# Two-block cached attention on one core: reciprocals by pairs of heads, K transposes behind them, another order of the PV evictions and exponentials, and a hinted branch at the end

## Chip, core and metric

The kernel runs on one core of a Trainium2 chip. The core has five engines: TensorE (PE; its weight loads are shown apart as PEld), VectorE (DVE), ScalarE (ACT), GpSimd (POOL) and SyncE (SP), and 16 DMA engines that move data between HBM and on-chip memory (SBUF). Results of TensorE land in PSUM, which has eight banks. The metric is the device time of one execution in microseconds (us). Before the change it is 743.23 us, the median of three runs (743.22 to 743.76).

## What is computed

Two blocks A and B of the same shape; each is a query projection, an attention over a cached K and V, and an output projection. The results stand side by side.

```python
def _A_ref(x, k_cache, v_cache, wq, wo):        # x 16x64x640, caches 16x32x512x128, wq 640x4096, wo 4096x640
    B, Sq, D = x.shape
    H, Dh = 32, 128
    q = (x @ wq).reshape(B, Sq, H, Dh).transpose(0, 2, 1, 3)
    scores = jnp.einsum("bhqd,bhkd->bhqk", q, k_cache) * (Dh ** -0.5)
    p = _softmax(scores, axis=-1)
    o = jnp.einsum("bhqk,bhkd->bhqd", p, v_cache)
    return o.transpose(0, 2, 1, 3).reshape(B, Sq, H * Dh) @ wo
...
return jnp.concatenate([a, b], axis=-1)          # 16 x 64 x 1280, bf16
```

## The kernel before

**Packs and phases.** The work is cut into 128 packs. A pack n is two batches (128 query rows) by four heads. Four packs make a group (16 heads of one pair of batches, sharing one transposed x and one accumulated output); eight groups (eight pairs of batches) make a phase; the four phases are block A heads 0 to 15, A heads 16 to 31, B heads 0 to 15, B heads 16 to 31. The last two packs are "narrow": their V is laid out in another way.

**The steps of one pack**, with the names that the planner uses: XT and XC (transpose of x, once per group), QP (query projection on PE, L610), QE (its eviction by ACT, L616), LDK and LDV (loads of K and V, issued by SP, L559 and L570), KT (two 32x32-block transposes of K by DVE, one for each half, L624), S (scores on PE, into the four PSUM banks 0 to 3, one for each head, L634), EX (exponential by ACT, one per head, which also writes the row sum, L653), RC (reciprocal of the row sums by DVE, L666), NM (normalisation of P by POOL, one per head, into `pn_sb`, L682), TR (transposes of P on PE, into banks 4 and 5, L693), TE (their eviction by DVE, one per bank, L703), PV (P times V on PE, into the first columns of banks 4 to 7, L716), OE (eviction of PV by ACT, in two halves: OE 0 reads banks 4 and 5, OE 1 reads banks 6 and 7, L724), ZO (ACT writes zeros over the part of banks 6 and 7 that PV used, L728), OP (output projection on PE, into the other columns of banks 6 and 7, L736), OS (DVE adds the group's sum, L746 and L749), ST (store of a finished group by ACT's queue, L755).

**What sets the order.** `build_plan` gives every step a due time in units of a pack, from the table `AT`; each engine's program is its steps sorted by due time. So one turn of PE is QP(n), PV(n-2), S(n), TR(n-1), OP(n-2), and DVE's turn before the change is

KT 0 (n), TE 0 (n-2), TE 1 (n-2), RC of heads 0 to 2 (n-1), KT 1 (n), RC of head 3 (n-1).

The loads on SP's queue are sorted by their own keys: V(n) is issued when PV(n-4) is done, since V has four buffers; K(m) has six buffers and stands about 2.5 packs further ahead. The waits between engines are worked out by the planner. Some steps of the other engines count on one semaphore that PE waits for (`for_pe`), and `stand_in` names, for every other dependence, a later step on the same engine whose completion covers it: before the change TR waits for the OE of banks 4 and 5, which stands second on ACT, and by that for both.

**The code on PE** is a loop over four packs; the other engines' programs are written out in full.

**The end.** The kernel computes the exponentials without subtracting the maximum. At the end DVE checks that all row sums are in range (FL1, FLM, FLC) and writes `flag`. Every engine loads the flag (L837) and branches (`If_ne`, L838): if it is not 128 the engine runs a second, general program, which lies behind the branch; otherwise it jumps over that program to the end, where ACT waits for the last store.

## Time and profile before

| what | value |
|---|---|
| median of three runs | 743.23 us |
| the profiled execution's own time | 743.14 us |
| its span, first to last instruction | 741.4 us |
| mean granted TensorE clock | 0.986 |
| busy DVE, ACT, POOL | 517.0, 519.8, 405.0 us |
| instructions | 61715 |
| DMA packets, bytes | 79841, 295.19 MB, mean 398 GB/s |

The span is the time that the trace covers; 1.7 us of the profiled execution's time lie around it. In the page, rows of busy shares cut the span into 40 equal slices (18.5 us each), a digit 9 standing for 90% or more. In the timeline, a row has the start and the length in us, the engine, the line of the kernel, the operation, output and input, and how many like instructions were merged; what stands in brackets is how long the engine was idle before and what released it. "SPq" is SP's queue, "PEldq" the sequencer of the engine.

### The profile page before, as it was taken

The page shows a single profiled execution, that of the slowest core. Times are in us where ns is not written, and L with a number is a line of the kernel's source. Part 1 is how long each engine was busy: PE and PEld are TensorE (multiplying, and loading weights), DVE is VectorE, ACT ScalarE, POOL GpSimd, SP SyncE. Part 2 cuts the span into 40 slices and gives each one's busy share as a digit, 9 for nine tenths or more (in the row PEclk, how much of TensorE's full clock was granted, in tenths as well). Part 3 has the DMA queues.
Part 4 walks back from the last instruction along what each step waited for, and adds up shares of the span by engine and source line. Part 5 has one row for each costly group of instructions (what it writes and reads, how often), then busy time and mean ns, then how long its engine had stood idle before and what let it go on. Part 6 is the DMA issues. An engine that isn't in the chain of part 4 may idle for free.

```text
span 741.4 us, 61715 instructions
## 1 busy us (share of the span) xinstructions
PE 680.6 (92%) x28502; PEld 532.2 (72%) x28502; DVE 517.0 (70%) x818; ACT 519.8 (70%) x1559; POOL 405.0 (55%) x580
## 2 busy tenths in 40 slices
PE   3679999999999999999988999999998899999995
PEld 2457777778787777777766777777776677777873
DVE  6347777778777776677755676677676677787874
ACT  1448787877777777776756777777776677777773
POOL 2635555555874544545674455455487455555551
PEclk9889999999999999999999999999999999999998
DMA  9999999999999999999999999999999999999980
GB/s 323 393 404 413 415 413 416 413 415 413 412 402 414 414 418 414 416 416 415 415 400 410 414 415 414 413 415 413 416 412 403 410 417 416 415 417 415 416 322 20
DMA packets 79841, 295.19 MB, mean 398 GB/s; under 512 B 13360, under 2 KB 28208, under 8 KB 63408
## 3 DMA queue, kind: packets, MB, share of 16 engines
q1 hardware_dynamic: 68384, 281.43, 93.9%
q10 hardware_dynamic: 11408, 13.27, 5.1%
q14 instruction: 39, 0.32, 0.1%
q8 instruction: 10, 0.16, 0.1%
HBM read 292.03 MB, written 2.62 MB: 397 GB/s over the span
## 4 chain that ended last, share of the span: by engine, by line
PE 45%; SPq 38%; DMA 7%; issue 4%; ACT 3%; POOL 2%; DVE 1%; ACTq 0%; DVEq 0%
SPq L559 24%; SPq L570 12%; PE ps L716 11%; PE ps L736 11%; PE ps L610 10%; PE ps L634 7%; PE ps L693 6%; DMA v_ring<-in_B_v_cache_dram 3%; DMA ws_sb<-in_A_wq_dram 2%; DMA kn_ring<-in_B_k_cache_dram 2%; ACT oT_sb L724 2%; SPq L544 1%; POOL pn_sb L682 1%; ACT ps L728 1%; POOL wqp_sb L582 1%
## 5 line engine op out<-in xcount | busy, mean ns | idle before, releaser
L682 POOL TENSOR_SCALAR pn_sb<-p_ring,recip 128x512 bf16<-128x512 bf16 x508 | 342.8, 696 | 304.1 <-DVE recip L666 304.1
L624 DVE STREAM_TRANSPOSE kt_ring<-kn_ring 128x1024 f32<-128x1024 f32 x256 | 312.0, 1227 | 105.3 <-DMA kn_ring<-in_B_k_cache_dram 69.7
L653 ACT ACTIVATE p_ring<-ps 128x512 bf16<-128x512 f32 x512 | 298.9, 598 | 35.3 <-issue 6.6
L703 DVE COPY pT_sb<-ps 128x1024 bf16<-128x1024 bf16 x258 | 164.4, 678 | 104.0 <-PE ps L693 103.5
L716 PE MATMUL ps<-pT_sb,v_ring 32*128 32x64 bf16 x16512 | 164.5, 192 | 18.6 <-DMA v_ring<-in_B_v_cache_dram 11.6
L716 PEld LDWEIGHTS ps<-pT_sb,v_ring 32*128 32x128 bf16 x16512 | 148.6, 91 | 34.0 <-DMA v_ring<-in_B_v_cache_dram 14.4
L610 PE MATMUL ps<-xT_ring,wqp_sb 128*128 128x128 bf16 x2560 | 165.8, 220 | 7.4 <-POOL xT_ring L599 7.1
L610 PEld LDWEIGHTS ps<-xT_ring,wqp_sb 128*128 128x128 bf16 x2560 | 157.2, 114 | 14.5 <-issue 7.3
L736 PE MATMUL ps<-wo_sb,oT_sb 128*128 128x320 bf16 x1040 | 166.3, 303 | 1.0 <-ACT ps L728 1.0
L724 ACT ACTIVATE oT_sb<-ps 128x256 bf16<-128x256 f32 x260 | 85.6, 381 | 108.9 <-PE ps L716 108.0
L634 PE MATMUL ps<-kt_ring,qs_ring 32*64 32x512 bf16 x4096 | 139.1, 382 | 3.7 <-issue 3.7
L693 PEld LDWEIGHTS ps<-ident,pn_sb 64*128 64x128 bf16 x4128 | 70.2, 95 | 76.6 <-ACT oT_sb L724 34.8
L616 ACT ACTIVATE qs_ring<-ps 128x512 bf16<-128x512 f32 x128 | 76.5, 598 | 62.3 <-PE ps L610 62.1
L736 PEld LDWEIGHTS ps<-wo_sb,oT_sb 128*128 128x128 bf16 x1040 | 92.0, 99 | 38.7 <-ACT ps L728 1.2
L653 ACT ACTIVATION_READ_ACCUMULATOR p_ring<-ps 128x1 f32 x512 | 106.1, 207 | 0.0
L693 PE MATMUL ps<-ident,pn_sb 64*128 64x64 bf16 x4128 | 84.1, 191 | 20.2 <-POOL pn_sb L682 6.7
L634 PEld LDWEIGHTS ps<-kt_ring,qs_ring 32*64 32x64 bf16 x4096 | 53.4, 103 | 32.1 <-issue 4.8
L728 ACT ACTIVATE ps<-zeros 128x256 f32<-128x256 bf16 x130 | 51.3, 394 | 0.0
L582 POOL COPY wqp_sb<-ws_sb 128x1280 bf16<-128x1280 bf16 x32 | 39.4, 1263 | 15.8 <-DMA ws_sb<-in_A_wq_dram 15.8
L666 DVE RECIPROCAL recip<-rowsum 128x3 f32<-128x3 f32 (+1 forms) x256 | 37.1, 145 | 5.3 <-ACT p_ring L653 0.7
L599 POOL COPY xT_ring<-xs_sb 128x640 bf16<-128x640 bf16 x32 | 23.1, 722 | 0.1
L589 PE MATMUL ps<-ident,xn_ring 128*128 128x128 bf16 x165 | 14.9, 222 | 3.9 <-DMA xn_ring<-in_A_x_dram 3.1
(26 smaller groups left out, 66.0 us busy)
## 6 DMA issues: line engine op xcount, KB each, us to landing
kn_ring<-in_A_k_cache_dram SPq DMA_DIRECT2D x256, 256.0 KB
v_ring<-in_A_v_cache_dram SPq DMA_DIRECT2D x128, 512.0 KB
kn_ring<-in_B_k_cache_dram SPq DMA_DIRECT2D x256, 256.0 KB
v_ring<-in_B_v_cache_dram SPq DMA_DIRECT2D x128, 512.0 KB
ws_sb<-in_B_wq_dram SPq DMA_DIRECT2D x10, 512.0 KB, 16.8
wo_sb<-in_B_wo_dram ACTq DMA_DIRECT2D x8, 640.0 KB, 13.5
ws_sb<-in_A_wq_dram ACTq DMA_DIRECT2D x4, 640.0 KB, 17.9
wo_sb<-in_A_wo_dram SPq DMA_DIRECT2D x4, 640.0 KB, 14.1
```

The source lines that it names most:

```text
L559: ins = e.dma_start(kn_ring[2 * b + l::4, n % NK].rearrange("p a c -> p (a c)"), src)
L570: ins = e.dma_start(dst.rearrange("p t d -> p (t d)"), src.rearrange("h (p t) d -> (h p) (t d)", t=16))
L610: last = e.matmul(ps[:, 1, f * 128:(f + 1) * 128], w[:, kt, f, :], xT_ring[:, xs, kt, :], start=(kt == 0), stop=(kt == KT - 1))
L624: ins = e.transpose(dst.rearrange("p c b (h l) -> p c h b l", h=8, l=2), src)
L634: last = e.matmul(ps[64 * b:64 * b + 64, i, :], qs_ring[rows, n % NQ, f, b, :], kt_ring[rows, n % NKT, :, f // 2, b, :, f % 2], start=(f = ...
L653: ins = e.activation(dst, src, ACTF.Exp, scale=1.0, accum_out=rowsum[:, h:h + 1])
L682: ins = e.tensor_scalar(dst, src, recip[:, h // 4 % NR, i:i + 1], 1.0, ALU.mult, ALU.mult)
L693: last = e.transpose(pt_bank(b)[:, 64 * c:64 * c + 64], pn_sb[rows, c, :], ident[rows, rows], tile_position=(64 * b, 0))
L703: ins = e.tensor_copy(pT_sb[:, b].rearrange("p t q -> p (t q)"), pt_bank(b))
L716: last = e.matmul(ps[:, 4 + i, 64 * b:64 * b + 64], v_ring[rows, n % NV, b, c, :], pT_sb[rows, b, c, :], start=(t == 0 and i < 2), stop=(t ...
L724: ins = e.activation(oT_sb[:, 2 * a:2 * a + 2, :], o_ps[:, 2 * a:2 * a + 2, :], ACTF.Copy)
L736: last = e.matmul(out_ps[:, s, :], oT_sb[:, i, :], wo_sb[:, 4 * j + i, s * NH0:(s + 1) * NH0], start=(j == 0 and i == 0), stop=(j == NJ - ...
```

## The change

- RC takes the heads in pairs, (0, 1) and (2, 3), in place of (0, 1, 2) and (3), and NM's dependence follows.
- The due times of RC go from (0.572, 0.794) to (0.45, 0.6), that of the second KT from -0.375 to -0.65. DVE's turn becomes KT 0 (n), KT 1 (n), TE 0 (n-2), RC of heads 0 and 1 (n-1), TE 1 (n-2), RC of heads 2 and 3 (n-1).
- EX of head 1 comes before that of head 0. Bank 1 is the one that QP of the next pack writes; bank 0 is the one that XT writes, once per group. The steps that PE waits for (`for_pe`) and the stand-ins follow this. The waits for the next x and for the reordered weights that hung on EX of head 0 are now behind the EX of head 1.
- OE 0 (banks 4 and 5, which TR writes next) comes before OE 1 (banks 6 and 7, which OP writes); OE 1 is stood in for by ZO.
- The final branch becomes `br_eq` with a hint. The place of the hint is marked 300 steps before the end of each engine's first program, and on PE behind its loop; one instruction is added to each engine there.

The instructions of the engines are otherwise the same in number and shape (RC has two columns in both, where it had three and one). SP's order of loads is the same.

```diff
-    AT = dict(XT=-2.585, XE=-2.383, XC=-0.788, QP=-0.428, QE=-0.224, KT=(-0.672, -0.375), S=0,
-              EX=(0.252, 0.307, 0.358, 0.616), RC=(0.572, 0.794), NM=(0.803, 0.854, 1.088, 1.187),
+    AT = dict(XT=-2.585, XE=-2.383, XC=-0.788, QP=-0.428, QE=-0.224, KT=(-0.672, -0.65), S=0,
+              EX=(0.307, 0.252, 0.358, 0.4), RC=(0.45, 0.6), NM=(0.803, 0.854, 1.088, 1.187),
...
-        add("act", "OE", (n, 1), n + AT["OE"][0], [], [("B67",), ("oT", 1)])
-        add("act", "OE", (n, 0), n + AT["OE"][1], [], [("B", 4), ("B", 5), ("oT", 0)])
+        add("act", "OE", (n, 0), n + AT["OE"][0], [], [("B", 4), ("B", 5), ("oT", 0)])
+        add("act", "OE", (n, 1), n + AT["OE"][1], [], [("B67",), ("oT", 1)])
...
-            add("dve", "RC", (n, a), n + AT["RC"][a], [("rs", 4 * n + i) for i in ((0, 1, 2), (3,))[a]],
+            add("dve", "RC", (n, a), n + AT["RC"][a], [("rs", 4 * n + i) for i in (2 * a, 2 * a + 1)],
...
     def for_pe(d):
         if d.kind == "EX":
-            return d.idx % 4 < 2
+            return d.idx % 4 == 1 or d.idx % 4 == 0 and d.idx // 4 % NJ == 1
...
             if d.kind == "OE":
-                return at[("OE", (d.idx[0], 0))]
+                return d if d.idx[1] == 0 else at[("ZO", d.idx[0])]
...
-            return at[("EX", d.idx // 4 * 4 + 2)]
+            alt = at[("EX", d.idx // 4 * 4)]
+            return at[("EX", d.idx // 4 * 4 + 2)] if for_pe(alt) else alt
...
-            lo, hi = ((0, 3), (3, 4))[a]
+            lo, hi = 2 * a, 2 * a + 2
...
-                for op in prog:
+                for i, op in enumerate(prog):
+                    if p == 0 and i == max(0, len(prog) - 300):
+                        ahead[eng] = e.mark_branch_hint_location()
                     emit(e, op, p, {})
...
+            if p == 0:
+                ahead[eng] = e.mark_branch_hint_location()
             for op in prog[lo + size * reps:]:
...
-                with e.If_ne(r, 128):
+                e.br_eq(r, 128, on_true=over, on_false=again).branch_hint(ahead[eng])
+                with nc.body(again, valid_engines=[e.engine]):
                     all_done(e, 0)
                     run_program(e, eng, 1)
                     if eng == "act":
                         all_done(e, 1, ("d_out",))
+                    e.br(over)
+                nc.switch_bb(over)
```

More of the change, by code (lines that the diff above doesn't have):

```diff
@@ L161, in build_plan @@
                 [("SB", i), ("p", h % cfg.NP), ("rs", h)])
-            add("pool" if n < N - 1 else "dve", "NM", h, n + (AT["NM"] if n < N - 1 else AT["NMZ"])[i], [("p", h % cfg.NP), ("recip", n % cfg.NR, i // 3)], [("pn", i)])
+            add("pool" if n < N - 1 else "dve", "NM", h, n + (AT["NM"] if n < N - 1 else AT["NMZ"])[i], [("p", h % cfg.NP), ("recip", n % cfg.NR, i // 2)], [("pn", i)])
         for a in range(2):
-            add("dve", "RC", (n, a), n + AT["RC"][a], [("rs", 4 * n + i) for i in ((0, 1, 2), (3,))[a]],
+            add("dve", "RC", (n, a), n + AT["RC"][a], [("rs", 4 * n + i) for i in (2 * a, 2 * a + 1)],
                 [("recip", n % cfg.NR, a)])
@@ L779, in mha_kernel @@
         emitters = {k[3:]: f for k, f in locals().items() if k.startswith("em_")}
+        ahead = {}
         def units(key):
@@ L835, in run @@
             e.wait_ge(sems[0][("s_flc_dve",)], 1)
+            again, over = "again_" + eng, "over_" + eng
             with e.register("flag_" + eng) as r:
                 e.reg_load(r, flag[0:1, 0:1])
-                with e.If_ne(r, 128):
+                e.br_eq(r, 128, on_true=over, on_false=again).branch_hint(ahead[eng])
+                with nc.body(again, valid_engines=[e.engine]):
                     all_done(e, 0)
```

## The prediction

> **What bounds the kernel now.** I read first the page's shares and slices, which show two resources near full at once.

> ```profile
> PE 680.6 (92%) x28502; PEld 532.2 (72%) x28502; DVE 517.0 (70%) x818; ACT 519.8 (70%) x1559; POOL 405.0 (55%) x580
> ...
> DMA  9999999999999999999999999999999999999980
> GB/s 323 393 404 413 415 413 416 413 415 413 412 402 414 414 418 414 416 416 415 415 400 410 414 415 414 413 415 413 416 412 403 410 417 416 415 417 415 416 322 20
> ```

> DMA moves about 415 GB/s from the fourth slice to the last but two; the dips (402, 400, 403) are the phase changes, when weights come too. In windows of 4 and 6 us the DMA share is 0.99 or more from 4 to 714 us. So until the loads run out no faster engine can bring data sooner. The chain of waits, in order of time, says where data stop deciding:

> ```profile
> 557.81 22.45 DMA v_ring<-in_B_v_cache_dram
> 580.30 1.74 PE ps L716 x114
> ...
> 692.33 1.25 PE ps L716 x128
> ```

> The chain's last DMA is the V that lands at 580.30 (PV of pack 98). From there PE leads to the end: pack 98 to pack 125 (723.49) in 143.19 us, 5.30 us a pack. Two things can therefore shorten the run: PE's cycle behind 580 us, and the end. The timeline shows the cycle:

> ```profile
> 700.57 1.29 DVE L703 COPY pT_sb<-ps 128x1024 bf16<-128x1024 bf16 x2 [0.79 <-PE ps L693]
> 701.96 0.18 DVE L666 RECIPROCAL recip<-rowsum 128x3 f32<-128x3 f32 x1
> 702.23 2.70 POOL L682 TENSOR_SCALAR pn_sb<-p_ring,recip 128x512 bf16<-128x512 bf16 x4 [2.73 <-DVE recip L666]
> 703.92 1.07 PE L634 MATMUL ps<-kt_ring,qs_ring 32*64 32x512 bf16 x32
> 705.07 0.64 PE L693 MATMUL ps<-ident,pn_sb 64*128 64x64 bf16 x32
> ...
> 707.27 2.70 POOL L682 TENSOR_SCALAR pn_sb<-p_ring,recip 128x512 bf16<-128x512 bf16 x4 [1.68 <-DVE recip L666]
> ...
> 709.10 1.07 PE L634 MATMUL ps<-kt_ring,qs_ring 32*64 32x512 bf16 x32
> ...
> 710.11 0.64 PE L693 MATMUL ps<-ident,pn_sb 64*128 64x64 bf16 x32
> ```

> The first TR starts 1.15 us behind its S, the second 1.01. The first waited for POOL: NM ends at 702.23 + 2.70 = 704.93, TR starts 0.14 later; NM could not start before RC, and RC not before three exponentials and both TE. PE's own work is done at S + 1.00. So PE's turn is 5.03 us, or 5.19 when NM is late; an XT adds 0.28 once in four.

> **The change part by part.** The sum starts from the profiled execution's own 743.14 us (span 741.40 and 1.74 around it), 0.09 under the median.

> *Reciprocals by pairs.* RC 0 waits for two exponentials and one TE. S ends about 0.13 us before EX starts; two exponentials and their sums take 0.57 x 2 + 0.2, so RC 0 starts 1.45 us behind S's end (705.0: 706.45), where it started at 707.00. NM follows about 0.55 us earlier, more than the 0.16 that TR waited. RC 1 (four exponentials, 705.12 + 4 x 0.57 + 0.2 = 707.6, plus 0.17) is there before NM's third head (706.7 + 2 x 0.68 = 708.05). TE 1 now stands behind RC 0 and ends about 0.15 us later, at 707.2; PV starts at 707.96, so 0.7 us cover it. From PV at 592.40 to the last S, the excess of S-to-TR over 1.00, summed over 26 packs, is 1.52 us. Term: -1.5. Bounds: 0 if the data cannot follow, -3.7 if PV also keeps to 1.21 us: in 14 of these packs it takes about 1.35, and the excess of PV-to-S over 1.14 sums to 2.2.

> *OE 0 first.* TR waits for one OE, not two: 0.33 us earlier (half of the pair's 0.66). In full packs the wait is hidden by S: OE 0 ended at 704.73 of the pair's 704.07 + 0.66, TR could start at 705.0. In the last pack there is no S: TR starts 0.72 behind the first OE (729.05, 729.77), then 0.39. PV of pack 126 gets the RC between its two TE, +0.1. Term: -0.2, bounds 0 and -0.33.

> *K transposes together.* DVE's turn is 2 x 1.22 + 1.29 + 2 x 0.17 = 4.1 of 5.03 us; from RC 1's end (707.8) the two KT end at 710.3, and TE is due at 710.79. So 0.5 us cover it, if K is there; with OS (0.8) the cover is nil. Where data decide, K is late and TE is behind it:

> ```profile
> 576.71 1.25 DVE L624 STREAM_TRANSPOSE kt_ring<-kn_ring 128x1024 f32<-128x1024 f32 x1 [3.65 <-DMA kn_ring<-in_B_k_cache_dram]
> ...
> 577.88 1.25 DVE L703 COPY pT_sb<-ps 128x1024 bf16<-128x1024 bf16 x2
> ...
> 580.30 1.74 PE L716 MATMUL ps<-pT_sb,v_ring 32*128 32x64 bf16 x128 [2.26 <-DMA v_ring<-in_B_v_cache_dram]
> ```

> TE would be done 2.45 + 1.3 + 0.3 = 4.05 us behind K's landing at 576.70, so PV at 580.75: V's landing (580.3) covers all but 0.45 us. That happens in up to 65 packs (the waits of DVE for K: 40 and 25). SP issues V when a PV is done, so 0.45 later too; what hides this is DMA's backlog:

> ```profile
> ws_sb<-in_B_wq_dram SPq DMA_DIRECT2D x10, 512.0 KB, 16.8
> wo_sb<-in_B_wo_dram ACTq DMA_DIRECT2D x8, 640.0 KB, 13.5
> ...
> xn_ring<-in_A_x_dram ACTq DMA_DIRECT2D x1, 160.0 KB, 2.1
> ```

> A transfer issued in the busy time lands 13 to 17 us later, one issued at the start 2.1: so more than 10 us of work are queued, and 0.45 us cannot empty that. Were the cover gone it would cost 65 x 0.45 = 29 us. Pack 98 starts 0.45 later; by pack 100 (its K at 588.27, PV at 592.3 against 592.40) this is made up. Term: 0, bounds 0 and +0.5.

> *EX of head 1 first.* QP starts after OP, 0.3 us behind the end of the second exponential; the swap only widens that. The waits for x (6.0 us in 7 packs) move one exponential back and still hold RC 0. SP's order of loads, POOL's and ACT's numbers of instructions stay. Term 0.

> *The hinted branch.* All engines branch at 736.8 to 737.1:

> ```profile
> L838 SPq COMPARE_BRANCH  x1: 50/50/50, 736.8 to 736.8; - x1
> ...
> L838 PEldq COMPARE_BRANCH  x1: 4182/4182/4182, 736.9 to 736.9; - x1
> ...
> L460 PEldq DRAIN  x1: 73/73/73, 741.1 to 741.1; - x1
> ```

> PE sits in the branch for 4.18 us; SP's next instruction comes 3.1 us behind its branch. Nothing is waited for there but the code at the target. A branch whose target is there costs 0.16 us (ACT's second one, 740.61 to its drain at 740.77). If the hint brings the code, the last store decides: issued at 736.25, landed by the row of the same 160 KB 2.1 us later, 738.35, then 0.16 and the 0.29 from PE's drain to the end of the span: 738.80 instead of 741.40. No row shows a hint. Bounds: -2.6 and, if the hinted fetch takes the place of code needed sooner, the +3.7 of the longest "issue" piece of the chain (27.30). I take -2.6: the 3 to 4 us are there on all five engines, and the hints stand 9 us ahead on PE (behind its loop, 727.6) and 180 us or more on the others (300 steps; ACT does 8 or 9 a pack).

> [...]

> Sum: 743.14 - 1.5 - 0.2 - 2.6 = 738.8 us.

> **The rivals.** (1) *The change doesn't do what it says: the hint brings no code*, or one engine's misses, and PE alone holds the end. For: no row shows one; five engines must all hit. Against: the target is known ahead. 738.8 + 2.6 = 741.4.

> (2) *Data, not PE, set the stretch behind 580.* At 416 GB/s a pack's 2.097 MB of K and V and its share of the store (0.04) take 5.14 us; PE's turn would be 5.03 + 0.28/4 = 5.10. For: that is almost equal. Against: behind 588.27 DVE never waits for K, and the DMA share falls to 0.74 from 714 us, as loads wait for V buffers, so data are ahead. The 1.5 are not won: 740.3.

> (3) *Slower: PE's clock falls.* The granted clock was 0.88 and 0.84 in the windows from 576 to 588 us, behind a gap of 2.26 us; after gaps of 1.59 (393.75, 572.94) it stayed at 1.00. The change adds 0.45 us to such gaps where K is late, as TE stands behind two KT. Each fall costs some 1.7 us (3.4 us at half speed). If, with PE faster than its data, four more gaps cross 2.26 us behind 580, where nothing makes it good: 738.8 + 4 x 1.7 = 745.6. It decides where gaps pass about 2 us. Against: a difference of 0.04 us a pack makes no such gaps. [...]

> (4) *PV also speeds up* to 1.21 us in the 14 packs, as the two KT lie elsewhere: 738.8 - 2.2 = 736.6. I know no reason for the 1.35.

> **How the numbers follow.** Forecast 0.48, rival 1 0.16, rival 2 0.16, rival 3 0.13, rival 4 0.07. A measurement can tell about 0.2%, 1.5 us, from no change: faster means under 741.7. Forecast, rivals 2 and 4 are faster; rival 1 lies at the bound, half of it counted as the same: faster 0.79, same 0.08, slower 0.13. The range reaches from 736.0, 0.6 below rival 4, to 742.7, all but the 742.9 of rivals 1 and 2 together (only the 0.2 won); it leaves out rival 3 and little else.

> **What would show it.** In the changed profile TR starts 1.00 us behind S in all packs of the last stretch, and no turn takes 5.19 us without an XT; POOL's NM starts before TE 1 ends; PE's final branch takes under 1 us and the drains come before 739 us, ACT's last. Wrong it would be if PE's branch still takes 4 us, if DVE waits for K behind 592 us, or if the granted clock is halved again between 590 and 730 us.

## The result, and the profile after

The changed kernel takes 741.74 us (median of 12 runs, 741.46 to 742.78); the kernel before, on the same chip, 743.33 us (12 runs, 742.85 to 744.09). The ratio is 0.9979, 95% interval 0.9970 to 0.9988: 1.6 us faster, where 4.4 were forecast. The profiled span went from 741.4 to 740.3 us. In the changed file the lines of the steps stand one further down: PV is L717, KT L625, RC L667, EX L654.

The page's shares and slices of the changed kernel, to be held against those of before:

```profile
PE 679.0 (92%) x28502; PEld 532.7 (72%) x28502; DVE 527.6 (71%) x818; ACT 530.1 (72%) x1559; POOL 404.8 (55%) x580
...
DMA  8999999999999999999999999999999999999980
GB/s 324 393 402 405 414 414 415 414 415 414 414 403 410 415 416 416 415 417 415 415 403 406 414 414 414 413 414 414 415 413 403 410 416 415 416 416 416 416 344 31
```

The DMA rows do not tell the two kernels apart: DMA is full to the last but two slices in both. DVE and ACT are busy some 10 us longer with the same number of instructions. The difference in time is in the two places that the prediction worked on. First the end. The instructions of the final branch's line, and two of the end's line, of the changed kernel (count, shortest/median/longest in ns, first and last start in us):

```profile
L846 SPq COMPARE_BRANCH  x1: 70/70/70, 738.6 to 738.6; - x1
...
L846 PEldq COMPARE_BRANCH  x1: 479/479/479, 738.7 to 738.7; - x1
```
```profile
L461 PEldq DRAIN  x1: 8/8/8, 739.3 to 739.3; - x1
...
L461 ACTq COMPARE_BRANCH  x1: 53/53/53, 739.9 to 739.9; - x1
```

PE's branch takes 0.48 us where it took 4.18; the drains of the other engines come at 739.1 to 739.3, and ACT's, which waits for the last store, is last. From the write of `flag` to the end of the span it was 5.27 us (736.13 to 741.40), now it is 2.32 (737.95 to 740.27): 2.95 us won, 2.6 forecast.

But the flag itself comes 1.8 us *later* than before, where 1.7 earlier was forecast. An ordinary turn behind 615 us, from the changed kernel's timeline:

```profile
702.99 0.17 DVE L667 RECIPROCAL recip<-rowsum 128x2 f32<-128x2 f32 x1
703.07 0.67 DVE L704 COPY pT_sb<-ps 128x1024 bf16<-128x1024 bf16 x1
703.24 2.69 POOL L683 TENSOR_SCALAR pn_sb<-p_ring,recip 128x512 bf16<-128x512 bf16 x4 [2.52 <-DVE recip L667]
...
704.37 1.22 PE L717 MATMUL ps<-pT_sb,v_ring 32*128 32x64 bf16 x128
705.51 1.07 PE L635 MATMUL ps<-kt_ring,qs_ring 32*64 32x512 bf16 x32
706.52 0.64 PE L694 MATMUL ps<-ident,pn_sb 64*128 64x64 bf16 x32
```

This is what the change promised: NM (703.24) starts before TE 1 ends (703.74), TR starts 1.01 us behind S, PV takes 1.22 us, and the turn is PE's own 5.03. But for a few with a longer PV, three turns of four are now like this. The fourth, the one with an XT, is not. The chain of waits (start, length, what it is) says where:

```profile
693.56 1.20 PE ps L717 x128
695.84 1.85 ACT p_ring L654 x6
699.34 1.21 PE ps L717 x128
...
714.50 1.20 PE ps L717 x128
716.78 1.85 ACT p_ring L654 x6
720.28 1.21 PE ps L717 x128
```

Once in four packs the chain leaves PE for *six* instructions of ACT: three exponentials and their sums. The timeline of the changed kernel there:

```profile
717.94 0.60 ACT L654 ACTIVATE p_ring<-ps 128x512 bf16<-128x512 f32 x1
...
718.41 0.21 ACT L654 ACTIVATION_READ_ACCUMULATOR p_ring<-ps 128x1 f32 x1
...
718.66 0.17 DVE L667 RECIPROCAL recip<-rowsum 128x2 f32<-128x2 f32 x1 [0.70 <-ACT p_ring L654]
718.74 0.67 DVE L704 COPY pT_sb<-ps 128x1024 bf16<-128x1024 bf16 x1
...
719.33 0.81 DVE L750 TENSOR_TENSOR out_sb<-acc,ps 128x640 bf16<-128x640 f32 x1
...
720.28 1.21 PE L717 MATMUL ps<-pT_sb,v_ring 32*128 32x64 bf16 x128 [0.48 <-DVE out_sb L750]
```

and of the kernel before, in the same pack:

```profile
715.97 1.29 DVE L703 COPY pT_sb<-ps 128x1024 bf16<-128x1024 bf16 x2 [1.29 <-PE ps L693]
...
717.22 0.17 DVE L666 RECIPROCAL recip<-rowsum 128x3 f32<-128x3 f32 x1
...
717.32 0.81 DVE L749 TENSOR_TENSOR out_sb<-acc,ps 128x640 bf16<-128x640 f32 x1
...
718.46 1.21 PE L716 MATMUL ps<-pT_sb,v_ring 32*128 32x64 bf16 x128
```

After the change the first RC waits until 718.62, the end of the third exponential's sum. TE 1 stands behind that RC, OS behind TE 1, and PV(124) waits 0.48 us for OS. Before, both TE and OS were done 0.3 us ahead of PV. The reason is in `stand_in`: in packs with n % 4 == 1 the exponential of head 0 counts on PE's own semaphore (XT needs its bank), so DVE's dependence on it is stood in for by the exponential of head 2. In these packs a pair of heads waits for three exponentials. The turn takes 5.85 us, where it took 5.46 to 5.60, and 5.31 would be PE's own pace.

Where the time went, from PV's starts in the two timelines (us; PV(n) is the first matmul of pack n's PV; PV(97) starts 0.65 us later after the change than before):

| stretch | before | after | after less before |
|---|---|---|---|
| PV(97) to PV(100), the hand-over from data to PE | 19.46 | 20.25 | +0.79 |
| PV(98) to PV(100), both starting at 580.3 | 12.10 | 13.52 | +1.42 |
| PV(100) to PV(124) | 126.06 | 126.44 | +0.38 |
| PV(124) to `flag` | 17.67 | 17.67 | 0 |
| `flag` to the end of the span | 5.27 | 2.32 | -2.95 |

PV(98) starts at 580.30 and 580.32; with these 0.02 us the rows below the first add up to the span's difference, -1.13. In the profile of before the granted clock was halved for 3.41 us of the hand-over (580.53 to 583.94), in that of the change it was not, so the rows of the hand-over show less than the change costs there.

### The profile page after: what moved, and what is told of

Same layout as the page of the kernel before. It is cut to its first block, busy times and chain, and to the rows that moved or that the text cites. A ratio compares the mean times of both kernels' runs of the same rounds, so it can differ in the third digit from the quotient of the medians.

```text
span 740.3 us, 61575 instructions
## 1 busy us (share of the span) xinstructions
PE 679.0 (92%) x28502; PEld 532.7 (72%) x28502; DVE 527.6 (71%) x818; ACT 530.1 (72%) x1559; POOL 404.8 (55%) x580
## 4 chain that ended last, share of the span: by engine, by line
PE 51%; SPq 20%; DMA 10%; ACT 9%; DVE 6%; issue 3%; POOL 1%; ACTq 0%; DVEq 0%
PE ps L717 15%; SPq L560 13%; PE ps L737 11%; PE ps L611 10%; PE ps L635 9%; ACT p_ring L654 6%; SPq L571 6%; PE ps L694 5%; DMA kn_ring<-in_B_k_cache_dram 5%; DMA wo_sb<-in_A_wo_dram 3%; DVE pT_sb L704 2%; ACT oT_sb L725 2%; DMA ws_sb<-in_A_wq_dram 2%; DVE out_sb L750 2%; ACT ps L729 1%
## 5 line engine op out<-in xcount | busy, mean ns | idle before, releaser
L625 DVE STREAM_TRANSPOSE kt_ring<-kn_ring 128x1024 f32<-128x1024 f32 x256 | 302.1, 1219 | 64.4 <-DMA kn_ring<-in_B_k_cache_dram 57.6
L654 ACT ACTIVATE p_ring<-ps 128x512 bf16<-128x512 f32 x512 | 298.4, 597 | 9.6 <-PE ps L635 4.8
L704 DVE COPY pT_sb<-ps 128x1024 bf16<-128x1024 bf16 x258 | 173.9, 675 | 82.3 <-PE ps L694 82.3
L717 PE MATMUL ps<-pT_sb,v_ring 32*128 32x64 bf16 x16512 | 165.3, 192 | 33.0 <-DVE pT_sb L704 12.6
L717 PEld LDWEIGHTS ps<-pT_sb,v_ring 32*128 32x128 bf16 x16512 | 149.9, 91 | 49.3 <-issue 31.7
L654 ACT ACTIVATION_READ_ACCUMULATOR p_ring<-ps 128x1 f32 x512 | 105.8, 207 | 0.0
L667 DVE RECIPROCAL recip<-rowsum 128x2 f32<-128x2 f32 x256 | 41.5, 162 | 58.8 <-ACT p_ring L654 50.1
## 6 DMA issues: line engine op xcount, KB each, us to landing
v_ring<-in_A_v_cache_dram SPq DMA_DIRECT2D x128, 512.0 KB
v_ring<-in_B_v_cache_dram SPq DMA_DIRECT2D x128, 512.0 KB
ws_sb<-in_B_wq_dram SPq DMA_DIRECT2D x10, 512.0 KB, 16.5
```

The lines of the kernel that those rows point to most:

```text
L625: ins = e.transpose(dst.rearrange("p c b (h l) -> p c h b l", h=8, l=2), src)
L654: ins = e.activation(dst, src, ACTF.Exp, scale=1.0, accum_out=rowsum[:, h:h + 1])
L704: ins = e.tensor_copy(pT_sb[:, b].rearrange("p t q -> p (t q)"), pt_bank(b))
L717: last = e.matmul(ps[:, 4 + i, 64 * b:64 * b + 64], v_ring[rows, n % NV, b, c, :], pT_sb[rows, b, c, :], start=(t == 0 and i < 2), stop=(t ...
```

## The experiments

Three theories. **W**: the loss in the body is the RC that waits for a third exponential, with TE 1, OS and PV behind it. **K**: it is the two K transposes side by side, behind which TE is late where K is late. **D**: data hold the stretch behind 594 us too (the prediction's second rival), so that no order of the engines wins much there. All runs of a group were made on one chip beside the kernel before; ratios are to it.

**The parts alone, and each suspect undone.** `h_only` is the kernel before with the hinted branch and nothing else:

```diff
-                with e.If_ne(r, 128):
+                e.br_eq(r, 128, on_true=over, on_false=again).branch_hint(ahead[eng])
```

> The kernel before with only the hinted branch. In the changed kernel's trace the stretch from the flag to the end of the span is 2.3 us where it was 5.3, and everything ahead of it is 1.8 us later than before. If these two are all there is, the hint alone gives 743.3 - 2.9 = 740.4 us, better than the whole change (741.7). If the hint also shifts code so that the body ahead of it changes, the time differs from 740.4 by more than 0.7.

`no_hint` is the change with the branch of before:

```diff
-                e.br_eq(r, 128, on_true=over, on_false=again).branch_hint(ahead[eng])
+                with e.If_ne(r, 128):
```

> The changed kernel with the end branch of before: all the reordering, no hint. By the same split 741.7 + 2.9 = 744.6 us, slower than before by 1.3. If the reordering itself is a gain, as forecast, it is below 742.5.

`te_first` makes the first RC due behind TE 1 in the packs with the third exponential:

```diff
-            add("dve", "RC", (n, a), n + AT["RC"][a], [("rs", 4 * n + i) for i in (2 * a, 2 * a + 1)],
+            add("dve", "RC", (n, a), n + (0.48 if n % NJ == 1 and a == 0 else AT["RC"][a]), [("rs", 4 * n + i) for i in (2 * a, 2 * a + 1)],
```

> The changed kernel, but in the pack behind each group's end (n mod 4 = 1) the first reciprocal stands behind the second TE and not between the two. Theory W: in that pack the reciprocal waits for the third exponential (its stand-in), the second TE, OS and PV wait behind it, and the turn takes 5.85 us in place of 5.31 to 5.46; behind 580 us there are seven such packs, 0.4 to 0.54 each: 738.0 to 739.0 us. Rival K: the loss comes from the two K transposes standing together (PV late where K lands late): unchanged, 741.7.

`kt_back` puts the second K transpose back where it was:

```diff
-    AT = dict(XT=-2.585, XE=-2.383, XC=-0.788, QP=-0.428, QE=-0.224, KT=(-0.672, -0.65), S=0,
+    AT = dict(XT=-2.585, XE=-2.383, XC=-0.788, QP=-0.428, QE=-0.224, KT=(-0.672, -0.375), S=0,
```

> The changed kernel with the second K transpose back at its due time of before (-0.375), now behind both reciprocals. Theory K: the 0.9 us that PV of pack 99 comes later is won back, and it is the main loss: 740.8 us or less. Theory W: the turns of 5.85 us stay, and S may wait for the second transpose: 741.0 to 742.2 us.

| kernel | median, us (lowest to highest, runs) | ratio, 95% interval |
|---|---|---|
| before | 743.41 (742.81 to 744.71, 20) | |
| h_only | 740.23 (739.78 to 740.83, 5) | 0.9958 (0.9944 to 0.9972) |
| no_hint | 744.78 (744.33 to 745.59, 11) | 1.0018 (1.0009 to 1.0027) |
| te_first | 740.63 (739.79 to 741.11, 5) | 0.9960 (0.9946 to 0.9973) |
| kt_back | 741.62 (740.70 to 742.55, 10) | 0.9975 (0.9966 to 0.9984) |

The hint alone is worth 3.2 us, more than the whole change; taken out of the change it costs 3.0 (744.78 less 741.74), and PE's branch takes 4.38 us again. All the reordering together is a loss of 1.4 us. Of W and K, W's repair brings 1.1 us and K's alone nothing that can be told. But W's repair stops well short of the 738.0 to 739.0 that W expected. In `te_first` the turns with an XT do fall, to 5.31 to 5.46 us, so the mechanism is gone; something else costs the kernel time then. Its waits between 594 and 718.5 us (engine, line and what it waited for: us in total, times, longest) name a candidate:

```profile
DVE recip L667 <- ACT p_ring L654: 7.4, 19, 0.4
DVE kt_ring L625 <- DMA kn_ring<-in_B_k_cache_dram: 3.5, 10, 0.7
```

DVE waits for K again, where the prediction relied on K being there behind 592 us. The trace's records of landings say it more sharply: in all 24 packs from 104 to 127 the first K transpose starts 0.02 to 0.17 us behind the last landing of its K.

**Both repairs; data out of the way.** `te_kt` has both edits above. `h_oe` is `h_only` with the change's order of OE (0 ahead of 1) and its stand-in. `te_less` is `te_first`, and `h_less` is `h_only`, with half of each V load left out from pack 100 on (that half of V is an older pack's):

```diff
+                f = 8 * DH if n >= 100 else 16 * DH
-                ins = e.dma_start(dst.rearrange("p t d -> p (t d)"), src.rearrange("h (p t) d -> (h p) (t d)", t=16))
+                ins = e.dma_start(dst.rearrange("p t d -> p (t d)")[:, :f], src.rearrange("h (p t) d -> (h p) (t d)", t=16)[:, :f])
```

> Both repairs at once: the first reciprocal pair of each group's second pack due ahead of the third exponential's stand-in (as in te_first, which took 1.1 us off the change), and the second K transpose back behind the second transposed-P copy (as in kt_back, alone no gain). The stretch behind 594 took 124.4 us up to PV(124) in te_first against 126.4 in the change; the hand-over PV(98) to PV(100) took 12.6 us in kt_back against 14.1 in te_first. If the two losses add up (theory W with K at the hand-over): 739.0 (738.4 to 739.5). If the data set the pace behind 580 (theory D; te_first's K transposes wait for K again in the last ten turns): no lower than te_first less its waits for K that the hand-over makes, 739.8 to 740.6.

> The kernel before with the hint and the order of the two PV-bank copies alone. The copies' order shortened the last turn from 3.97 to 3.70 us and lengthened the one ahead by 0.13 us in the change. Theory W and theory D alike: 740.1 (739.6 to 740.5), against 740.23 with the hint alone. If the order of the copies is what costs in the body: 741.0 or more.

> te_first with half of each V load left out from pack 100 on (half of V there is an older pack's; the output of those packs differs), so that some 1.57 MB a pack are loaded behind pack 100 in place of 2.10. Theory D: the waits for K behind 600 go, all turns but the group ends come to 5.03 and the group ends to 5.31, so PV(100) to PV(124) takes 122.4 us against 124.4: 738.6 (738.0 to 739.2). If data are not what lengthens te_first's turns: 740.6 as te_first.

> The kernel before with the hint, and with the same half of each V load left out from pack 100 on. The stall of transposes behind S (turns of 5.19 and 5.46) was put down to the order on ScalarE and VectorE, not to data. If so: the turns of 5.19 and 5.46 stay, 740.2 (739.6 to 740.6) as with the hint alone. If late K data made those turns too (theory D for the kernel before): they come to 5.03 and 5.31, PV(100) to PV(124) falls from 126.5 to 122.4 us, 736.5.

**The change itself, and both repairs, with the same half left out:** `after_less` and `kt_less`.

> The change itself, with half of each V load left out from pack 100 on (the output of those packs differs). Theory W (the group-end turns of 5.85 us come from the reciprocal that waits for the third exponential, not from data): the turns of 5.85 stay, PV(100) to PV(124) takes 6 x 20.94 = 125.6 us against 122.40 in te_less, so 3.2 us more than te_less's 737.8: 741.0 (740.3 to 741.7), hardly below the change with all its data. Theory D alone (late data made those turns long): 737.8 (737.0 to 738.5), as te_less.

> te_kt (both repairs), with the same half of each V load left out. Up to pack 99 nothing but the place of the second K transpose differs from te_less. If K's transposes together cost at the hand-over: PV(98) to PV(99) 6.5 to 6.7 us against 7.41 in te_less, 737.1 (736.5 to 737.5). If they cost nothing there and te_kt's gain over te_first came from elsewhere: 737.8.

| kernel | median, us (lowest to highest, runs) | ratio, 95% interval |
|---|---|---|
| before, beside the first four | 743.43 (743.21 to 744.39, 9) | |
| te_kt | 739.76 (739.70 to 739.95, 5) | 0.9950 (0.9936 to 0.9963) |
| h_oe | 740.34 (740.06 to 740.55, 5) | 0.9956 (0.9942 to 0.9970) |
| te_less | 737.80 (736.87 to 738.69, 5) | 0.9927 (0.9913 to 0.9940) |
| h_less | 738.31 (738.13 to 739.34, 5) | 0.9930 (0.9917 to 0.9944) |
| before, beside the last two | 743.81 (742.73 to 744.50, 9) | |
| after_less | 741.33 (740.74 to 742.33, 5) | 0.9965 (0.9951 to 0.9978) |
| kt_less | 736.59 (735.74 to 737.40, 4) | 0.9902 (0.9887 to 0.9917) |

With half of V gone the timelines become clean enough to add up. A stretch of 24 packs at PE's own pace is 18 turns of 5.03 and 6 of 5.31 (an XT), 122.40 us. Of each kernel, PV(100) to PV(124), and what lies over that: PV to S over 1.14 us (PV is long), S to TR over 1.00 (NM is late), and the turns with an XT over 5.31, less what the other two make of them (OS is late); what is left, within 0.25 us, is rounding.

| kernel | PV(100) to PV(124) | PV long | NM late | OS late | PV(124) at |
|---|---|---|---|---|---|
| before | 126.06 | 2.21 | 1.35 | 0 | 718.46 |
| h_only | 126.52 | 3.16 | 1.14 | 0 | 717.97 |
| after | 126.44 | 0.88 | 0.09 | 3.20 | 720.28 |
| te_first | 124.45 | 2.05 | 0.16 | 0 | 718.44 |
| te_kt | 125.02 | 2.64 | 0.17 | 0 | 717.97 |
| h_less | 124.31 | 0.12 | 1.95 | 0 | 717.54 |
| after_less | 125.65 | 0.09 | 0.07 | 3.19 | 720.62 |
| te_less | 122.40 | 0 | 0.24 | 0 | 715.09 |
| kt_less | 122.40 | 0 | 0 | 0 | 714.77 |

The stages PV(100) to PV(124) of `te_less` and of `after_less` (first and last us; length; busy us and instructions of PE, its weight loads, DVE, ACT, POOL; granted clock, DMA share, GB/s):

```profile
592.69:715.09 122.40, 122.40 (x5311) 96.79 (x5312) 97.08 (x151) 96.83 (x288) 68.70 (x103) 1.00 0.89 308
```
```profile
594.97:720.62 125.65, 122.82 (x5311) 97.02 (x5311) 96.88 (x151) 96.96 (x289) 68.71 (x102) 1.00 0.86 293
```

In `te_less` PE is busy for all 122.40 us. In `after_less`, with as little to load, PE stands still for 2.8 us, and the waits of that stretch name them (of the seven waits of PE the first lies ahead of the stretch):

```profile
DVE recip L669 <- ACT p_ring L656: 11.5, 24, 0.7
PE ps L719 <- DVE out_sb L752: 3.3, 7, 0.5
```

So W is shown apart from data: 3.2 us in this stretch, 6 turns of 0.54 us, as expected before the run (741.0 expected, 741.33 measured; without W 737.8). The loads cost the kernels without W something too: by the medians of their groups these fall by 1.9 us (`h_only` to `h_less`), 2.8 (`te_first` to `te_less`) and 3.2 (`te_kt` to `kt_less`) when half of V is not loaded, while the change falls by 0.4. But they do not cost it in the way that D says. The three columns make up all that lies over 122.40, and none is a wait that the profile puts down to data: in `te_first` DVE's waits for K do not reach PE, which is busy for all 124.40 us from 594.00 to 718.40. What goes with half of V is the long PV.

The late NM was real, and is the order's doing: it stays in `h_less` (1.95) and is gone in the kernels with RC by pairs. With all data `te_kt` and `te_first` take 1.5 and 2.1 us less than `h_only` from PV(100) to PV(124), but PV(100) itself starts 1.5 and 2.5 us later there, so that all three, and `before`, reach PV(124) within 0.5 us of each other. The granted clock was halved for 3.41 us ahead of PV(100) in these two and not in `h_only`, so single profiles do not say what part of that is the order's.

Not all forecasts held: `te_kt` came out between the ranges of W and D, `te_less` 0.2 us below its range, and `h_less` between its two forecasts, since its late NM stayed and its long PV went.

As for K: with data out of the way, up to pack 99 `kt_less` and `te_less` differ in the second K transpose alone. The expected gain did show in PV(98) to PV(99) (6.62 us against 7.41), but the turn ahead was longer by 0.86, so that PV(97) to PV(100) gained only 0.32. The clock was halved for 3.41 us there in `kt_less` and not in `te_less`, which may hide part of it. The medians differ by 1.2 us, with intervals that overlap.

**Loads of K earlier.** If late K were what costs these kernels time, K one pack further ahead in SP's queue would free the order's gain:

```diff
-    KLEAD = 2.5
+    KLEAD = 3.5
```

> te_kt with each pack's K loads one pack further ahead of the V loads in SyncE's queue (lead 3.5 packs in place of 2.5); the order on the other engines is the same. Theory D says that behind pack 100 it is K that lands late while V waits in its ring (no wait of TensorE for V there), so K one pack earlier takes the late K away: PV(100) to PV(124) falls from 125.0 us to 122.4, as with half of V left out: 737.3 (736.5 to 738.3). If the loads were fast enough, or if V then comes late by as much: 739.8 or more.

> The kernel before with the hint, and K's loads one pack further ahead as in te_kt_k35. Theory D: PV(100) to PV(124) falls from 126.5 to 124.3 us, the pace of its own order that h_less showed (turns of 5.03 and 5.19, group ends of 5.46), 738.9 (738.1 to 739.9), and te_kt_k35 beats it by about 1.9 us, the gain of the order that data hid. If data hide nothing: 740.2, and the two differ by 0.5 as they did with the lead of 2.5.

`te_kt_k35` took 741.82 us (740.01 to 742.88, 11 runs; ratio 0.9970, 0.9960 to 0.9980), `h_only_k35` 742.76 (741.72 to 743.64, 11 runs; 0.9992, 0.9983 to 1.0001), beside 743.41 (742.62 to 744.00, 21 runs): by the medians 2.1 and 2.5 us *slower* than with the lead of 2.5. The runs of `te_kt_k35` fall into two groups, five at 740.0 to 740.2 and six at 741.8 to 742.9; the profile is of the second. There K lands 5.2 to 6.4 us ahead of its first transpose in packs 104 to 127, and DVE waits for none. The stretch still takes 125.37 us, with 3.05 us of long PV; and PV comes 0.8 to 3.6 us later than in `te_kt` from pack 2 on. So PV is long with K on time too. What goes with a long PV can be seen beside SyncE's issues of K, in one turn of `te_kt` and one of `te_less`:

```profile
689.33 2.99 SPq L560 DMA_DIRECT2D kn_ring<-in_B_k_cache_dram  x4
...
691.84 1.34 PE L717 MATMUL ps<-pT_sb,v_ring 32*128 32x64 bf16 x128
```
```profile
686.50 2.38 SPq L560 DMA_DIRECT2D kn_ring<-in_B_k_cache_dram  x4
...
689.38 1.22 PE L719 MATMUL ps<-pT_sb,v_ring 32*128 32x64 bf16 x128
```

The same 128 matmuls take 0.12 us more, with no wait named, at the same granted clock (1.00), and in packs 108 to 125 of `te_kt` V had landed 2.0 us or more ahead of its PV. The matmuls are not slower throughout: they start some 8 ns apart, and in a long PV of `te_kt` they stop, mostly once, for 0.08 to 0.22 us. In the turn shown, the last issue of K in `te_kt` ends at 692.32, inside PV, and the stop ends 0.39 us later; in `te_less` it ends at 688.88, ahead of PV. This holds in all 14 traces, packs 100 to 125: 116 PV have a stop of over 0.07 us, and it ends 0.38 to 0.40 us behind the end of an issue of K in 113 of them, 0.29 to 0.30 us in the other three. Of the 116 issues of K for which that moment falls 0.56 us or more into a PV, 115 show the stop. In `te_less`, and in `no_hint` with all its data, the four issues of a pack take 2.4 us (median) and are over in time, and no PV stops; in `te_kt` they take 3.0 and run into the next PV. That the issue itself stops PE, and not something behind both, no run tests, and why the issues take longer stays open too.

## Why the prediction was wrong, by its own steps

By the profiles, the terms came out so: the hint -2.95 (-2.6 forecast); PV(100) to PV(124), where the reciprocals were to win 1.5, +0.38 (W costs 3.2, NM and PV give 1.3 each back, to within the rounding); the hand-over, where the K transposes were to cost nothing, +1.42; behind PV(124), where the order of OE was to win 0.2, 0.

**The failing step is the first term, "reciprocals by pairs", -1.5.** "RC 0 waits for two exponentials and one TE" holds in three packs of four. In the fourth it waits for three, by the stand-in that the diff shows, and it was costed from a pack where it doesn't. "PV starts at 707.96, so 0.7 us cover it" was read from an ordinary pack too: in the turn behind a group's last pack OS stands behind TE 1 as well. The prediction had said of DVE's turn, under another term, that "with OS (0.8) the cover is nil", and did not carry it over to this one. The price, 0.54 us over PE's own pace in 6 of 24 turns, is 3.2 us.

**The gain it set against that was there, and did not reach the time.** NM's lateness did go (1.35 to 0.09 us in the 24 packs; `te_kt` 0.17), and with half of V left out the order wins 1.9 us in the stretch (`h_less` 124.31, `kt_less` 122.40). With W repaired and all data, `te_first` takes 740.63 us and `te_kt` 739.76, beside the 740.23 of the hint alone. That is near the 740.3 of the prediction's rival 2, given 0.16, but not by its account: it has PE wait for loads at 5.14 us a pack, and `te_kt` takes 5.21 (125.02 over 24), with K and V landed ahead of use, PE all but always busy, and PV longer. That its number fits is luck. The argument against that rival, "behind 588.27 DVE never waits for K", holds but for one wait of 0.2 us, and by a small margin: in the profile of before, K lands 0.02 to 1.5 us ahead of its first transpose in packs 104 to 127, which the list of waits, showing only waits, could not tell. In the changed kernel DVE waits for K four times behind 592 us, 1.5 us in all, which the prediction had named as a sign of being wrong; the three columns above leave no time of PE to it.

**K transposes together, 0 (0 to +0.5), was too low at the hand-over.** There PV(97) to PV(100) takes 20.25 and 19.89 us in the two profiles with the two side by side and the clock at full (after, `te_less`), 18.91 with the order of before (`h_only`, `h_oe`). Where the clock is halved for 3.41 us it takes 20.82 to 21.41 with them side by side (`no_hint`, `te_first`, `after_less`), 19.43 to 20.08 with them apart (`before`, `h_less`, `kt_back`, `te_kt`, `kt_less`). So some 0.7 to 2.0 us, not 0.45 that is made up by pack 100. It can be seen in the changed kernel (the window of this view cuts the row of PV short):

```profile
583.93 2.37 DVE L625 STREAM_TRANSPOSE kt_ring<-kn_ring 128x1024 f32<-128x1024 f32 x2 [3.68 <-DMA kn_ring<-in_B_k_cache_dram]
...
586.22 0.65 DVE L704 COPY pT_sb<-ps 128x1024 bf16<-128x1024 bf16 x1
...
587.68 1.22 PE L717 MATMUL ps<-pT_sb,v_ring 32*128 32x64 bf16 x115 [2.20 <-DVE pT_sb L704]
```

Both transposes wait for K, TE 0 for both, and PV for TE, no longer for V. By the medians, putting the second one back is worth 0.1 us in the change (`kt_back`), 0.9 beside `te_first` (`te_kt`) and 1.2 with half of V left out (`kt_less`), with intervals that overlap each time.

**OE 0 first, -0.2: won in one place and lost in two.** PV(126) to PV(127) went from 3.97 to 3.70 us. PV(125) to PV(126) went from 4.42 to 4.55 (the forecast +0.1), and PV(127) to `flag` from 4.25 to 4.39: there ZO, and OP behind it, start 0.14 us later behind the pair of OE, which the term left out. Together that is 0. In `h_oe`, with the order of OE alone, 0.14 us are won behind PV(124); by the median it is not faster than `h_only`.

**EX of head 1 first, 0:** the term belongs to W. Before, the exponentials of heads 0 and 1 counted on PE's semaphore in every pack, so an RC of these two would have waited for the third exponential each time. With head 1 first, head 0's counts there in packs with n % 4 == 1 alone; these are the packs in which the pair still waits for three.

**The hinted branch, -2.6: right, a little low.** 2.95 in the profiles, 3.2 by `h_only`. Rival 1 fell, and its 741.4 us is near the result by chance only.

**Rival 3, a falling clock, did not come about** behind 592 us: the change's granted clock is 1.00 from there to 740. Rival 4 did, in part: PV to S over 1.14 fell from 2.21 to 0.88 us. That is not because the K transposes lie elsewhere: `kt_back`, where they are apart, has 0.91. It goes with SyncE's four issues of K in a pack, which take 2.7 us (median) in the change and 3.1 before, and so end inside fewer PV (5 with a stop in packs 100 to 125, 14 before); in `te_kt`, without W, 2.64 us are back.

## What to carry to other kernels

A wait that moves earlier on average can move later in one turn of four. Cost a reordering by going through every kind of turn of the period, with the stand-ins as they come out in each, and name what is queued behind the waiting instruction there: here 0.16 us was won in some turns, and every fourth went from 5.46 to 5.85.

Here PE was the bound and DMA full as well (a share of 1.02 from 600 to 710 us in `te_kt`), and leaving half of V out took 3.2 us off `te_kt` (739.76 to 736.59), though no wait of PE for data is listed there from 593 to 718 us. In such a case compare landing and use (K's slack was at most 1.5 us before and 0.17 in `te_first`), leave out half of one load, and look inside a group of instructions that grew longer for what happens on the other queues at that moment.

The branch over the second program at the end cost 4.18 us on PE here, and 0.48 with the hint; it is cheap to look for: a branch of some us with no wait named. The best version here takes the hint and both repairs (`te_kt`, 739.76 us); the hint alone (740.23) has nearly all of it, and the intervals of the two overlap.

## What the runs showed of the hardware

**With the hint the last branch was short.** PE's branch took 4.18 us (before) and 4.38 (`no_hint`), with the hint 0.48 (the change and `h_only` alike); the drains of SP, POOL and DVE came 3.2 to 3.5 us behind their branches before and 0.5 to 0.6 us in the change. That it is the code at the target which the branch waited for is the author's reading: the hinted branch alone makes the difference in these runs, and no row names what is waited for.

```profile
580.00:590.00 10.00, 7.74 (x372) 6.04 (x367) 5.03 (x8) 4.94 (x15) 4.59 (x7) 0.87 1.03 414
```
```profile
580.00:590.00 10.00, 7.74 (x365) 5.77 (x352) 5.46 (x8) 5.63 (x17) 4.19 (x7) 1.00 1.04 411
```

Of 14 profiles, 10 have a window of 3.41 us at half clock between 578 and 592 us, with gaps of 1.77 to 2.44 us; 4 have none, with gaps of 1.68 to 2.28. So the length of such a gap does not decide alone. The prediction's "about 2 us", which lay between the 1.59 and the 2.26 of one trace, was no bound, and what else decides no run shows.

**PV's matmuls stopped where an issue of K ended beside them,** 0.38 to 0.40 us behind the end of SyncE's issue in 113 of 116 cases, for 0.08 to 0.22 us. The 128 matmuls then took mostly 0.11 to 0.16 us more: in 15 of 24 turns of `te_kt`, and in none with half of V left out. Which of the two causes it, the issue or something behind both, was not tested.
